# Opening of a fused attention and feed-forward kernel: QKV weight slices in column halves, row 0's mean from two partial sums, rows 1 and 2 turned elsewhere, one residual load moved

## The chip, the cores and the metric

The kernel runs on one core of a Trainium2 chip. A core has TensorE (PE, with its weight loads shown apart as PEld), VectorE (DVE), ScalarE (ACT), GpSimd (POOL) and SyncE (SP), which issues most DMAs; ACT can issue DMAs too. The metric is the device time of one execution in microseconds (us), here the median of three runs.

## The reference, cut to what matters

```python
xn = (x - mean(x)) / sqrt(var(x) + 1e-5)            # x: 2048 x 576, bf16
q, k, v = split(xn @ wqkv)                          # wqkv: 576 x 1728; 32 heads of 18
logits = [q[s] . k[s - 2 w] for w in range(8)] * 18 ** -0.5   # masked where s < 2 w
o = sum(softmax(logits)[w] * v[s - 2 w])
out = x + o @ wo + (silu(xn @ w_gate) * (xn @ w_up)) @ w_down # F = 4608
```

## The kernel before, in words

The 2048 tokens are 16 rows of 128 tokens (token = 16 * partition + row), in four quarters of four rows. The order of all instructions of an engine is the order in which the code issues them (`manual_schedule`); waits between engines are put in by the framework from what each instruction reads and writes.

**Loads (L144 to L165).** `wqkv` is cut along the contraction into slices 0 to 3 of 128 rows and slice 4 of 64 rows, which is kept in two halves of columns, one on partitions 0 to 63, one on 64 to 127. ACT issues row 0 of x and slice 1; SP issues row 1, slice 0, slice 2, row 2, slice 3, slice 4 (two loads), row 3, and then x's chunks 1, 2 and 3 of four rows each (L165). x's chunks lie in the space of `wd`, the QKV weights in that of `hT` (the profile names them so).

**Warm-up (L171).** `warm_pe(n, m)` issues n matmuls of 512 columns and m of 128 on constants. ACT runs a Sqrt ahead (L166), which brings its table load early.

**Layer norm.** `ln_half` (L214) takes bn_stats of 288 of a row's 576 elements, `ln_aggr` (L218) makes mean and variance of both halves, `ln_sqrt` (ACT, L229) and `ln_recip` (L234) the reciprocal deviation, `ln_apply` (L240) the normalized row; POOL or DVE appends a copy of the last 64 elements (L243, L246), so that a row is five tiles of 128. Row 0 is special: it is only centred (`ln_center`, L251; POOL's pad, L256), and its deviation is multiplied in when the products are taken out of PSUM (L365, L367). It is normalized as well, into `xn0`, for later use, and that copy is turned by DMA.

**Turning.** A row's five tiles are transposed by TensorE. For rows 0 and 1 this is `transp_pe` (L262) into PSUM tiles `pa`, `pb` (and `pt1`, the warm-up's bank), copied to SBUF by `copy_pt` (L268). For rows 2 to 4 `transp_halves` (L283, copied at L287) is put in the middle of the matmuls of the row before; later rows are turned by DMA (L291).

**QKV.** A row's products are four PSUM tiles of 432 columns. Row 0 goes slice by slice (`p_whole`, L301): 4 matmuls on slice 0, 4 on slice 1, two on slice 2, then row 1's first three transposes, the other two on slice 2, row 1's last two transposes, then row 1's 4 matmuls on slice 0, and row 0's on slices 3 and 4 (`p_row0_rest`). Later rows use `p_row`: matmuls of half height, two at a time on the two halves of the array, in two passes (`swap`); `at=(i, kt)` says after which step of the second pass the next row is turned. `p_evac` takes the products out, shared between ACT and DVE (L363 to L367).

**After that.** From 60.0 us on, each quarter (`tt`) runs nine chunks (`ch`) of gate and up projections (`g_pair`, L601) with weights `gu` loaded two chunks ahead into two buffers; DVE works on a quarter's attention from a queue of pieces with costs in us (`Filler`). Then come the down projection and `wo` (L630), the residual `xr` is added (L642), and the row is stored. `xr` is loaded at the end of chunk 7 as two DMAs of two rows (L674); `store(2, 3, 3)` writes a buffer of V out in three DMAs at the end of chunk 0 of quarter 0 (L671).

Of the kernel before, what the change touches and what calls it, by code (L numbers as in the profile page):

```python
# [9 lines left out]
bf16 = mybir.dt.bfloat16  # L10
f32 = mybir.dt.float32
ACT = mybir.ActivationFunctionType
ALU = mybir.AluOpType
# [57 lines left out]
def kernel(  # L71
# [75 lines left out]
    def load_w(eng, kt):  # L147
        if kt < 4:
            eng.dma_start(wqkv[:, kt, :], A_wqkv[kt * P:(kt + 1) * P, :])
        else:  # L150
            for i in range(2):
                eng.dma_start(wqkvr[64 * i:64 * i + 64, :], A_wqkv[4 * P:D, 2 * G * i:2 * G * (i + 1)])

    load_x(nc.scalar, 0)
    load_x(nc.sync, 1)
    load_w(nc.scalar, 1)
    load_w(nc.sync, 0)
    make_identity(nc, ident[:])
    load_w(nc.sync, 2)
    load_x(nc.sync, 2)  # L160
    load_w(nc.sync, 3)
    load_w(nc.sync, 4)
    load_x(nc.sync, 3)
    for c in range(1, 4):
        nc.sync.dma_start(xc_b[c], x_v[:, 4 * c:4 * c + 4, :])  # L165
    nc.scalar.activation(warm[:], eps_t[:], ACT.Sqrt)  # L166

    wp = ps.tile([P, 512], f32, name="warm_ps", tag="ps")
    pt1 = wp[:].bitcast(bf16)

    def warm_pe(n, m):  # L171
        one = lambda shape: nc.const_aps.tensor(1.0, shape, bf16)
        for i in range(n):
            nc.tensor.matmul(wp[:].rearrange("p (a b) -> p a b", b=P), one([P, P]), one([P, 4, P]),  # L174
                             start=True, stop=True)
        for i in range(m):
            nc.tensor.matmul(wp[:, 0:P], one([P, P]), one([P, P]), start=True, stop=True)  # L177
# [27 lines left out]
        ln[c] = (xc_b[c], xn_b[c % 2], mv, rstd)  # L205

    sums = {}

    def ln_half(r, k):
        c, j = divmod(r, 4)  # L210
        xc, xn, mv, rstd = ln[c]
        if k == 0:
            sums[r] = lns.tile([P, 2, 6], f32, name="stats")
        nc.vector.bn_stats(sums[r][:, k, :], xc[:, j, k * HALF:(k + 1) * HALF])  # L214

    def ln_aggr(r):
        c, j = divmod(r, 4)
        nc.vector.bn_aggr(ln[c][2][:, j, :], sums[r][:].rearrange("p c s -> p (c s)"))  # L218

    def ln_stats(r, n=1):  # L220
        for i in range(r, r + n):
            ln_half(i, 0)
            ln_half(i, 1)
            ln_aggr(i)

    def ln_sqrt(r, n=1):
        c, j = divmod(r, 4)
        xc, xn, mv, rstd = ln[c]
        nc.scalar.activation(rstd[:, j:j + n], mv[:, j:j + n, 1], ACT.Sqrt, bias=eps_t[:], scale=1.0)  # L229

    def ln_recip(r, n=1):
        c, j = divmod(r, 4)
        rstd = ln[c][3]
        nc.vector.reciprocal(rstd[:, j:j + n], rstd[:, j:j + n])  # L234

    def ln_apply(r):
        c, j = divmod(r, 4)
        xc, xn, mv, rstd = ln[c]
        dst = xn[:, j] if r else xn0
        nc.vector.tensor_scalar(dst[:, 0:D], xc[:, j], mv[:, j, 0:1], rstd[:, j:j + 1],  # L240
                                op0=ALU.subtract, op1=ALU.mult)
        if r < 2:
            nc.gpsimd.tensor_scalar(dst[:, D:DPAD], xc[:, j, 512:D], mv[:, j, 0:1], rstd[:, j:j + 1],  # L243
                                    op0=ALU.subtract, op1=ALU.mult)
        else:
            nc.vector.tensor_copy(dst[:, D:DPAD], dst[:, 512:D])  # L246

    def ln_center(r, lo=0, hi=D):
        c, j = divmod(r, 4)
        xc, xn, mv, rstd = ln[c]  # L250
        nc.vector.tensor_scalar(xn[:, j, lo:hi], xc[:, j, lo:hi], mv[:, j, 0:1], None, op0=ALU.subtract)  # L251

    def ln_center_pad(r):
        c, j = divmod(r, 4)
        xc, xn, mv, rstd = ln[c]
        nc.gpsimd.tensor_scalar(xn[:, j, D:DPAD], xc[:, j, 512:D], mv[:, j, 0:1], None, op0=ALU.subtract)  # L256

    def transp_pe(r, kts, pt):
        c, j = divmod(r, 4)
        xn = ln[c][1]  # L260
        for i, kt in enumerate(kts):
            nc.tensor.transpose(pt[:, i * P:(i + 1) * P], xn[:, j, kt * P:(kt + 1) * P], ident[:])  # L262
# [4 lines left out]
    def copy_pt(eng, r, kts, pt):  # L267
        eng(xT_of(r)[:, kts[0]:kts[-1] + 1, :],  # L268
            pt[:, 0:len(kts) * P].rearrange("p (k t) -> p k t", t=P))
# [34 lines left out]
    def p_whole(r, t, kt, gs=range(NG)):  # L304
        for g in gs:
            p_mm(t, g, kt, None, r, kt == 0, False)
# [14 lines left out]
    def p_row(r, between=None, at=(0, 1), t=None):  # L321


        done = t is not None
        t = t or [None] * NG
        fence = {}
        for swap in range(2):
            for i in range(2):
                for kt in (0, 1, 2, 3) if swap else (0, 4, 1, 2, 3):
                    if done and kt == 0:  # L330
                        continue
                    for half in range(2):
                        g = i + 2 * (half ^ swap)
                        if t[g] is None:
                            t[g] = new_ps("qkv_ps")
                        mm = p_mm(t, g, kt, half, r, swap == 0 and kt == 0, swap == 1 and kt == 3)
                        if swap == 0 and kt == 3 and half == 1:
                            fence[i] = fence_after(mm)
                        if swap and kt == (1 if done else 0) and half == 0:
                            fence_before(mm, fence[i])  # L340
                    if swap and (i, kt) == at and between is not None:
                        between()
        return t
# [36 lines left out]
    def store(m, c, parts=1):  # L380
        st = stage[(2 * c + m - 1) % 4].rearrange("p r d -> p (r d)")
        n = XC // parts
        for i in range(0, XC, n):
            nc.sync.dma_start(kv_d[m - 1, c - 1, :, i:i + n], st[:, i:i + n])
# [89 lines left out]
    def turn(r):  # L474
        return lambda: transp_halves(r)

    warm_pe(10, 1)
    ln_open(0)
    ln_stats(0)
    ln_center_pad(0)  # L480
    ln_center(0, 0, P)
    ln_sqrt(0)
    pa, pb = new_pt(), new_pt()
    transp_pe(0, (0,), pa)
    ln_center(0, P, D)
# [3 lines left out]
    ln_stats(1)  # L489
    ln_sqrt(1)  # L490
    copy_pt(nc.scalar.copy, 0, (3, 4), pb[:, 2 * P:])
    ln_recip(0)
    ln_apply(0)
    ln_recip(1)
    ln_apply(1)

    t = [new_ps("qkv_ps") for g in range(NG)]
    p_whole(0, t, 0)
    p_whole(0, t, 1)
    p_whole(0, t, 2, (0, 1))  # L500
    transp_pe(1, (0, 1), pt1)
    transp_pe(1, (2,), pa)
    copy_pt(nc.scalar.copy, 1, (0, 1), pt1)
    copy_pt(nc.vector.tensor_copy, 1, (2,), pa)
    p_whole(0, t, 2, (2, 3))
    transp_pe(1, (3, 4), pb)
    copy_pt(nc.scalar.copy, 1, (3, 4), pb)
    u = [None] * NG
    for g in (0, 2, 1, 3):
        u[g] = new_ps("qkv_ps")  # L510
        p_whole(1, u, 0, (g,))
    p_whole(0, t, 3)
    p_row0_rest(t)
    ln_stats(2)
    ln_sqrt(2)
    normalize(2)
    p_evac(0, t, (5, 0, 3, 2, 4, 1), dve=(5, 2))
    ln_half(3, 0)
# [1 line left out]
    load_gu(0)  # L520
    transp_dma(0)

    p_row(1, turn(2), (0, 2), u)
    ln_aggr(3)
    p_evac(1, u, (0, 1, 2), dve=(1, 2))
    ln_sqrt(3)
# [120 lines left out]
    for tt in range(NTT):  # L647
        for ch in range(NCH):
            it = tt * NCH + ch
            for p in range(2):  # L650
                g_pair(tt, ch, p)
                for j in (2 * p, 2 * p + 1):
                    g_evac(ch, j)
                    if it % NCH < NCH - 1 or p == 0:
                        dve.pump(1.4)
            if ch == NCH - 1:
                dve.drain(lambda: chains[0] > tt)
                for r in range(RT * tt, RT * tt + RT):
                    nc.sync.dma_start_transpose(oT[:, :, r * P:(r + 1) * P], QOP[:, r, :])
            if it + NSLOT < NTT * NCH:  # L660
                load_gu(it + NSLOT)
            if tt == 0:
                if 1 <= ch <= 7:
                    load_wd(ch - 1)
                if ch == 5:
                    load_wd(8)
                for _ in range(3 if ch in (1, 2) else 2):
                    if wo_order:
                        load_wo(wo_order.pop(0))
                if ch == 0:  # L670
                    store(2, 3, 3)  # L671
            if ch == 7:
                for i in (0, 2):
                    nc.sync.dma_start(xr[:, i:i + 2, :], x_v[:, RT * tt + i:RT * tt + i + 2, :])  # L674
            if ch == 1 and tt < NTT - 1:
                chain(tt + 1)
        for sub in range(0, RT, 2):
            t, fence = {}, {}
            for swap in range(2):
                for i in (sub, sub + 1):  # L680
                    d_half(tt, i, swap, t, fence)
                    if swap:
                        dve.pump(12.5 if i == sub else 4.0)
                        d_out(RT * tt + i, i, t[i])
# [30 lines left out]
```

## Time and profile before

| What | us |
|---|---|
| median of three runs | 504.54 (503.37 to 505.05) |
| the profiled execution, in all | 503.82 |
| its span (first to last instruction) | 502.0 |
| PE busy | 498.1 (99%) |
| PE on gate and up (L601) | 280.4 |
| PE on down projection and wo (L630) | 146.9 + 23.4 |
| PE on QKV, half-height matmuls and others (L301) | 50.2 |
| PE on the warm-up (L174) | 4.4 |
| first matmul on real data (L262, L301) | starts at 5.21, 6.06 |

How to read it: an engine's busy time is the time in which one of its instructions runs. Matmuls overlap, and their ends are modelled, so where PE is busy throughout, the starts of single matmuls say more than the busy share. The chain of waits is followed back from the last instruction. In a timeline, a row is start, length, engine, line, operation, tiles written and read, and in brackets how long the engine had been idle and what released it. In the stretches view, PEclk is the granted clock, the last two columns are the busy share of the DMA engines and what they moved in GB/s.

### The profile page before, as it was taken

What the parts mean: (1) busy time and instruction counts of PE and PEld (TensorE: products, weight loads), DVE (VectorE), ACT (ScalarE), POOL (GpSimd) and SP (SyncE); (2) the same over time, 40 slices, a digit from 0 to 9 for tenths busy, and PEclk for the clock granted to TensorE, in tenths of its full rate; (3) what the DMA queues carried; (4) which work ended last, traced back from release to release, by engine and by line L of the source; (5) the groups of instructions that cost most, each with busy time, mean ns of one, the idle gap of its engine ahead of it and who ended that gap; (6) DMA issues with size and microseconds to landing.
All of it is one profiled execution on the core that took longest, in us unless ns stands there. A gap on an engine that the chain in (4) does not pass through costs nothing.

```text
span 502.0 us, 13267 instructions
## 1 busy us (share of the span) xinstructions
PE 498.1 (99%) x5795; PEld 330.5 (66%) x5795; DVE 329.0 (66%) x478; ACT 200.5 (40%) x415; POOL 2.6 (1%) x9
## 2 busy tenths in 40 slices
PE   9999999999999999999999999999999999999997
PEld 4666655555799755555899655555999555557996
DVE  5888598898999698999898139995980222221001
ACT  4756657644400255554300445557000454553000
POOL 2000000000000000000000000000000000000000
PEclk9999999999999999999999999999999999999999
DMA  8889988789921045536621154465600335453100
GB/s 313 219 206 228 307 280 280 220 273 309 233 82 61 25 136 193 191 106 225 161 69 43 29 185 146 139 189 157 136 25 14 100 114 178 155 177 38 29 14 25
DMA packets 77186, 75.42 MB, mean 150 GB/s; under 512 B 22708, under 2 KB 72528, under 8 KB 77128
## 3 DMA queue, kind: packets, MB, share of 16 engines
q1 hardware_dynamic: 76840, 73.98, 49.7%
q8 instruction: 45, 0.74, 0.6%
q10 hardware_dynamic: 288, 0.59, 0.4%
q14 instruction: 13, 0.11, 0.1%
HBM read 58.76 MB, written 5.90 MB: 129 GB/s over the span
## 4 chain that ended last, share of the span: by engine, by line
PE 99%; DVE 0%; issue 0%
PE g_ps L601 56%; PE d_ps L630 32%; PE qkv_ps L301 11%; PE warm_ps L174 1%; PE pt L262 0%; DVE ot L644 0%; PE pt L283 0%; PE warm_ps L262 0%; PE warm_ps L177 0%
## 5 line engine op out<-in xcount | busy, mean ns | idle before, releaser
L601 PE MATMUL g_ps<-xnT,gu 64*128 64x512 bf16 x2592 | 280.4, 376 | 0.0
L601 PEld LDWEIGHTS <-gu 64*128 64x128 bf16 x2592 | 147.7, 94 | 131.3
L612 ACT ACTIVATE sg<-g_ps 128x512 bf16<-128x512 f32 x144 | 87.3, 606 | 156.6 <-PE g_ps L601 156.6
L630 PE MATMUL d_ps<-wd,hT 64*128 64x288 bf16 x2304 | 146.9, 283 | 0.0
L630 PEld LDWEIGHTS <-hT 64*128 64x128 bf16 x2304 | 131.3, 94 | 10.5
L614 DVE TENSOR_TENSOR hT<-sg,uc 128x512 bf16<-128x512 bf16 x144 | 60.0, 418 | 93.8 <-ACT uc L613 93.6
L613 ACT CAST uc<-g_ps 128x512 bf16<-128x512 f32 x144 | 85.2, 592 | 0.0
L414 DVE TENSOR_REDUCE PP<-PP 128x64 f32<-128x1152 bf16 x64 | 84.9, 1345 | 0.4
L301 PE MATMUL qkv_ps<-hT,xnT 64*128 64x432 bf16 (+1 forms) x536 | 50.2, 343 | 0.0
L409 DVE TENSOR_TENSOR PP<-QO,Kr 128x2304 bf16<-128x2304 bf16 (+1 forms) x35 | 43.5, 1249 | 7.2 <-DMA Kr<-hT 6.9
L642 DVE TENSOR_TENSOR ot<-d_ps,xr 128x288 bf16<-128x288 f32 x30 | 12.3, 451 | 51.1 <-PE d_ps L630 51.1
L441 DVE TENSOR_TENSOR PP<-Vr,A 128x2304 bf16<-128x2304 bf16 (+1 forms) x35 | 43.2, 1250 | 0.4
L301 PEld LDWEIGHTS <-xnT 64*128 64x128 bf16 (+1 forms) x536 | 30.1, 94 | 18.5 <-ACT xnT L287 0.4
L446 DVE TENSOR_TENSOR PP<-PP 128x2304 bf16<-128x2304 bf16 x24 | 32.5, 1353 | 0.3
L612 ACT ACT_TABLE_LOAD x5 | 6.4, 1283 | 47.3 <-PE g_ps L601 47.2
L630 PE MATMUL d_ps<-wo,xnT 64*128 64x288 bf16 x288 | 23.4, 283 | 0.0
L363 ACT CAST hT<-qkv_ps 128x288 bf16<-128x288 f32 (+2 forms) x58 | 21.2, 428 | 0.5 <-DMA kv_d<-hT 0.5
L630 PEld LDWEIGHTS <-xnT 64*128 64x128 bf16 x288 | 16.4, 94 | 1.2
L434 ACT ACTIVATE PP<-PP 128x1024 f32<-128x1024 f32 x4 | 4.2, 1057 | 31.2 <-DVE PP L430 31.2
L644 ACT CAST ot<-d_ps 128x288 bf16<-128x288 f32 x1 | 0.4, 399 | 38.8 <-PE d_ps L630 38.8
L363 ACT CAST QO<-qkv_ps 128x432 bf16<-128x432 f32 (+1 forms) x30 | 12.3, 410 | 7.4 <-PE qkv_ps L301 7.4
L214 DVE BATCH_NORM_STATS2 stats<-wd 128x6 f32<-128x288 bf16 x32 | 12.9, 444 | 2.9 <-DMA wd<-in_A_x_dram 2.6
(53 smaller groups left out, 91.3 us busy)
## 6 DMA issues: line engine op xcount, KB each, us to landing
gu<-in_B_w_gate_dram SPq DMA_DIRECT2D x36, 512.0 KB, 3.8
gu<-in_B_w_up_dram SPq DMA_DIRECT2D x36, 512.0 KB, 5.1
wd<-in_B_w_down_dram SPq DMA_DIRECT2D x9, 576.0 KB, 6.0
kv_d<-hT SPq DMA_DIRECT2D x5, 576.0 KB, 6.4
gu<-in_B_w_gate_dram SPq DMA_DIRECT2D x36, 64.0 KB, 4.7
gu<-in_B_w_up_dram SPq DMA_DIRECT2D x36, 64.0 KB, 4.4
xr<-in_A_x_dram SPq DMA_DIRECT2D x8, 288.0 KB, 5.1
out_dram<-ot SPq DMA_DIRECT2D x16, 144.0 KB, 1.8
```

The costliest lines, as they stand in the source:

```text
L214: nc.vector.bn_stats(sums[r][:, k, :], xc[:, j, k * HALF:(k + 1) * HALF])
L301: return nc.tensor.matmul(t[g][:, 0:G], xT_of(r)[rows, kt, :], w_at(g, kt, rows), start=start, stop=stop)
L363: (nc.vector.tensor_copy if n in dve else nc.scalar.copy)(*parts[n])
L409: nc.vector.tensor_tensor(prod[:, a:b], QO[:, RT * tt + a:RT * tt + b, :], Kr[:, s:s + b - a, :], op=ALU.mult)
L414: nc.vector.tensor_reduce(L[:, w, rs], prod[:, rs].rearrange("p r (h d) -> p r h d", d=DH), axis=AX.X, op=ALU.add)
L441: nc.vector.tensor_tensor(dst[:, a:b], Vr[:, s:s + b - a, :].rearrange("p r (d h) -> p r d h", h=H), A[:, w, a:b].unsqueeze(2).to_broadcas ...
L446: nc.vector.tensor_tensor(dst, acc, pv, op=ALU.add)
L601: mm = nc.tensor.matmul(ring_ps[j][b][:], gu[rows, slot, k, fc], xnT[rows, kt, tok], start=(swap == 0 and kt == 0), stop=(swap == 1 and kt ...
L612: nc.scalar.activation(sg[:], t[0][:], ACT.Silu)
L613: nc.scalar.copy(uc[:], t[1][:])
L614: nc.vector.tensor_tensor(hT[:, ch * FC + j, :], sg[:], uc[:], op=ALU.mult)
L630: mm = nc.tensor.matmul(t[sub][h][:, 0:HALF], a[rows], w[rows, h * HALF:(h + 1) * HALF], start=(swap == 0 and n == 0), stop=(swap == 1 and ...
```

## The change

- Slices 0, 1 and 2 of `wqkv` are each loaded as two DMAs of 128 rows by 864 columns, the left half issued by SP, the right half by ACT, in the order 0, 1, 2. Slice 3, slice 4 and the rows stay on SP. x's chunks 2 and 3 come in one DMA.
- Row 0's mean: ACT copies the left half of the row with a factor 1/576 and sums it, DVE does the same with the right half (`ln_mean0`; the copies go to a scratch area); the centring subtracts both sums. The bn_stats of row 0 (`ln_half(0, ...)`, `ln_aggr(0)`), its Sqrt, reciprocal and normalizing come later, behind row 1's.
- One warm-up matmul of 512 columns less.
- Row 1's transposes: three after row 0's slice 1, all into `pb`, two after three of the four matmuls on slice 2; all its copies on ACT. `ln_stats(2)` and `ln_sqrt(2)` come sooner. Row 2 is turned one step sooner in row 1's second pass.
- Quarter 0's residual is loaded as one DMA of four rows at the end of chunk 0; V's last buffer is stored in two DMAs there instead of three.

```diff
     load_x(nc.scalar, 0)
     load_x(nc.sync, 1)
-    load_w(nc.scalar, 1)
-    load_w(nc.sync, 0)
+    for kt in range(3):
+        for eng, cols in ((nc.scalar, slice(2 * G, 4 * G)), (nc.sync, slice(0, 2 * G))):
+            eng.dma_start(wqkv[:, kt, cols], A_wqkv[kt * P:(kt + 1) * P, cols])
     make_identity(nc, ident[:])
-    load_w(nc.sync, 2)
     load_x(nc.sync, 2)
     load_w(nc.sync, 3)
     load_w(nc.sync, 4)
     load_x(nc.sync, 3)
-    for c in range(1, 4):
-        nc.sync.dma_start(xc_b[c], x_v[:, 4 * c:4 * c + 4, :])
+    nc.sync.dma_start(xc_b[1], x_v[:, 4:8, :])
+    nc.sync.dma_start(wdf[:, 2 * XC:4 * XC].rearrange("p (r d) -> p r d", d=D), x_v[:, 8:16, :])
...
+    def ln_mean0():
+        xc = ln[0][0]
+        nc.scalar.activation(PP[:, 1, 0:HALF], xc[:, 0, 0:HALF], ACT.Copy, scale=1.0 / D, accum_out=part[:, 0:1])
+        nc.vector.tensor_scalar(PP[:, 1, HALF:D], xc[:, 0, HALF:D], 1.0 / D, None,
+                                op0=ALU.mult, op1=ALU.add, accum_out=part[:, 1:2])
...
-        nc.vector.tensor_scalar(xn[:, j, lo:hi], xc[:, j, lo:hi], mv[:, j, 0:1], None, op0=ALU.subtract)
+        nc.vector.tensor_scalar(xn[:, j, lo:hi], xc[:, j, lo:hi], part[:, 0:1], part[:, 1:2],
+                                op0=ALU.subtract, op1=ALU.subtract)
...
-    warm_pe(10, 1)
+    warm_pe(9, 1)
     ln_open(0)
-    ln_stats(0)
+    ln_mean0()
     ln_center_pad(0)
     ln_center(0, 0, P)
-    ln_sqrt(0)
...
     copy_pt(nc.scalar.copy, 0, (3, 4), pb[:, 2 * P:])
-    ln_recip(0)
-    ln_apply(0)
+    ln_half(0, 0)
     ln_recip(1)
     ln_apply(1)
+    ln_half(0, 1)
+    ln_aggr(0)
 
     t = [new_ps("qkv_ps") for g in range(NG)]
     p_whole(0, t, 0)
     p_whole(0, t, 1)
-    p_whole(0, t, 2, (0, 1))
-    transp_pe(1, (0, 1), pt1)
-    transp_pe(1, (2,), pa)
-    copy_pt(nc.scalar.copy, 1, (0, 1), pt1)
-    copy_pt(nc.vector.tensor_copy, 1, (2,), pa)
-    p_whole(0, t, 2, (2, 3))
-    transp_pe(1, (3, 4), pb)
-    copy_pt(nc.scalar.copy, 1, (3, 4), pb)
+    transp_pe(1, (0, 1, 2), pb)
+    copy_pt(nc.scalar.copy, 1, (0,), pb)
+    copy_pt(nc.scalar.copy, 1, (1, 2), pb[:, P:])
+    p_whole(0, t, 2, (0, 1, 2))
+    transp_pe(1, (3, 4), pb[:, 3 * P:])
+    copy_pt(nc.scalar.copy, 1, (3, 4), pb[:, 3 * P:])
+    p_whole(0, t, 2, (3,))
+    ln_sqrt(0)
+    ln_stats(2)
+    ln_sqrt(2)
+    ln_recip(0)
+    ln_apply(0)
...
     p_row0_rest(t)
-    ln_stats(2)
-    ln_sqrt(2)
     normalize(2)
...
-    p_row(1, turn(2), (0, 2), u)
+    p_row(1, turn(2), (0, 1), u)
...
-                    store(2, 3, 3)
-            if ch == 7:
-                for i in (0, 2):
-                    nc.sync.dma_start(xr[:, i:i + 2, :], x_v[:, RT * tt + i:RT * tt + i + 2, :])
+                    store(2, 3, 2)
+            if ch == (7 if tt else 0):
+                n = 2 if tt else RT
+                for i in range(0, RT, n):
+                    nc.sync.dma_start(xr[:, i:i + n, :], x_v[:, RT * tt + i:RT * tt + i + n, :])
```

## The prediction

> **What bounds the kernel now.** I read the page's busy times first, then what TensorE waited for, then the chain that ended last, then the first 16 us engine by engine.
>
> ```profile
> PE 498.1 (99%) x5795; PEld 330.5 (66%) x5795; DVE 329.0 (66%) x478; ACT 200.5 (40%) x415; POOL 2.6 (1%) x9
> ...
> PE 99%; DVE 0%; issue 0%
> ```
>
> PE is busy through the span and is 99% of the chain. Its ends are modelled, so "busy" can hide small stalls; I therefore read the starts of single matmuls in the trace. From 13.93 us to the end no matmul starts more than 0.06 us after the columns of the one before it have passed. The rest of the kernel is thus a fixed sum of matmuls: the change can gain only ahead of 13.93, and must not open a hole behind it. The chain of waits for the first 20 us, start and length:
>
> ```profile
> 0.76 4.42 PE warm_ps L174 x10
> 5.18 0.11 PE warm_ps L177
> 5.29 0.21 PE pt L262
> 5.50 0.02 issue
> 5.52 0.61 PE pt L262 x4
> 6.13 2.25 PE qkv_ps L301 x10
> ```
>
> Real work begins at 6.06 (the first L301). All before it is warm-up and the turning of row 0. The timeline says what row 0 waits for (start, length, instruction):
>
> ```profile
> 3.81 0.82 DVE L214 BATCH_NORM_STATS2 stats<-wd 128x6 f32<-128x288 bf16 x2 [2.63 <-DMA wd<-in_A_x_dram]
> 4.66 0.21 DVE L218 BATCH_NORM_AGGREGATE mv<-stats 128x2 f32<-128x12 f32 x1
> 4.90 0.56 DVE L251 TENSOR_SCALAR wd<-wd,mv 128x128 bf16<-128x128 bf16 x2
> 5.21 0.91 PE L262 MATMUL pt<-ident,wd 128*128 128x128 bf16 x5
> 5.54 0.27 ACT L268 COPY PP<-pt 128x128 bf16<-128x128 bf16 x1 [0.34 <-PE pt L262]
> 6.06 2.31 PE L301 MATMUL qkv_ps<-hT,PP 128*128 128x432 bf16 x10
> ```
>
> Row 0 of x lands at 3.78 (the trace's semaphore times), and the chain is stats, aggregate, centre, turn, copy. The copied tile is loaded into PE at 5.85, yet the matmul starts at 6.06, because slice 0 lands at 6.02. So two things release row 0: this chain and slice 0. The other landings: slice 1 5.74, slice 2 7.16, row 2 7.59, slice 3 9.09, slice 4's halves 9.57 and 9.83. After 6.06, PE loses 0.10 at 8.95 (copies of row 1), 0.10 at 10.52 (the step to half-height matmuls), and 0.14 at 13.73, where weight loads wait for row 2's turned tile:
>
> ```profile
> 13.70 0.51 PEld L301 LDWEIGHTS <-xnT 64*128 64x128 bf16 x8 [0.37 <-ACT xnT L287]
> ```
>
> It also loses to a slow start: warm-up matmuls of 512 columns start 0.427 apart and row 0's first three 0.31 and 0.36 apart, but from 6.93 on 432 columns take 0.182. So PE runs at half its later rate until about 6.7, although the stretches view gives a granted clock of 1.00 there.
>
> **Row 0's mean.** ACT now issues four loads instead of two; an issue takes 0.46 (plus 0.03), so its table load (1.28) moves from 1.64 to about 2.62 and the warm Sqrt ends near 4.12. Starts on ACT overlap by 0.1, so its half of the sum starts at 4.02, not at 3.81. I take 0.40 for it (256-column copies on L268 take 0.35 to 0.37). Writing the sum out is not in this trace: between nothing and one more small ACTIVATE (L229: 0.29); I take 0.15, near the 0.11 to 0.15 of L234. The DVE half (a bn_stats of 288 takes 0.45) is done before. The centring starts at 4.62 instead of 4.90: **0.28 sooner** (0.13 to 0.43). Two scalars instead of one cost nothing there: 576 columns with two (L240) take 0.43, 448 with one 0.39. One warm-up matmul less ends the warm-up at 4.71, before the centring's 4.87, so it hides nothing and costs nothing. Turning and copying follow as before: tile loaded at 5.57, PE free of the other four transposes at about 5.64, first L301 at **5.67, 0.39 sooner, if slice 0 is there**.
>
> **Slices in halves.** The same bytes, slice 0 first instead of 0 and 1 together. In the trace's packets, full-height 3456 B pieces take 135 ns each on a DMA engine, and the first 1728 B pieces 72 ns (later ones 114, below). Per engine, slice 0 is then 16 x 72 = 1.15 us instead of the 2.16 us that slices 0 and 1 take: it lands at 6.02 - 1.01 = 5.01, in time. Slice 1 lands at 6.17 (used from 6.93), slice 2 at 7.38 (used at 7.83). All behind is 3 x 0.072 = 0.22 later: slice 3 at 9.31, slice 4 at **10.05**. An issue waits for the landing of the one eight before it (the semaphore numbers repeat after eight), so SP issues row 2 at 3.8, slice 3 at 4.2, slice 4 at 5.0 and 5.6, row 3 at 6.2, x's chunks at 6.8 and 7.4. Since data flows until 7 by then, the DMA engines do not run dry; behind, gu's first loads start within 0.5 of before, and are used at 60.0. Chunk 2 now lands with chunk 3 (14.5 instead of 13.1), and is read only after row 7's normalizing.
>
> **Row 0 and 1 on PE.** I leave the change of rate at 6.7, since the first warm-up matmul stays at 0.76; at half rate until then, a 0.39 earlier start is worth 0.195. Row 1 is applied by 7.16 and padded by 7.62; PE asks for it at 7.66 and 8.38 (before: 8.21), so turning it sooner costs no stall here. Its copies then lie beside slice 2's three matmuls (0.55), so the 0.10 at 8.95 goes. All three copies are on ACT now, then two Sqrt (0.29 each); row 0's rstd is ready near 9.5 and wanted at 10.2. Slice 3's matmuls start at 9.40 (landed 9.31), slice 4's at 10.23 (landed 10.05) instead of 10.52: **0.29 gained**, with slack of 0.1 and 0.2 left. So slice 4 is next late: even a free row 0 could not bring more than 10.52 - 10.05 = 0.47.
>
> **Row 2 turned one step sooner**: one pair of half-height matmuls (0.183) more lies between its transposes and row 2's first matmul; the stall of 0.137 goes. Its two banks are freed by ACT's copies near 11.9 and wanted at 12.06. **0.14 gained.**
>
> **Residual in the first chunk**: one load of 576 KB at about 72 us instead of two in chunk 7, one store fewer. In the stretches view the DMA engines idle there (75 to 76: share 0.07, 25 GB/s), and gu's next load, issued at 75.8 and landed by 81.3, is wanted at 83.2. Cost 0; without that hole it would take 1.5 of a slack of 1.9.
>
> **Sum**, against the profiled execution (span 502.0, 503.82 in all): 0.195 + 0.095 + 0.14 = 0.43 us, to 503.39. The median of the three runs is 0.72 above it, so 504.54 - 0.43 = **504.1**. At most 0.47 + 0.14 = 0.6; with both bounds of the ACT sum 0.3 to 0.5.
>
> The Trainium skill's "TensorE: Matmul & The Clock Gate", in "Part 1: The HAM clock gate", says the half rate ends at the edge of a free-running window of about 3.4 us, so not by work done. The change of rate 6.0 us after the first matmul allows that (two such windows are an estimate of at most 6.8), and by that rule 0.195 stands; were the rate bound to row 0's third matmul, as the trace allows too, the sum would be 0.39 + 0.095, capped at 0.47, plus 0.14: 0.6.
>
> **Rivals.**
> 1. *Slower: the halves move slowly.* From 8 to 9 us, while slice 4's 1728 B pieces were in flight, the DMA engines were full and moved little (GB/s is the last column):
>
> ```profile
> 7.00:7.50 0.50, 0.50 (x5) 0.25 (x4) 0.43 (x1) 0.02 (x1) 0.50 (x2) 1.00 1.06 415
> 8.00:8.50 0.50, 0.50 (x7) 0.36 (x5) 0.00 (x0) 0.00 (x0) 0.00 (x0) 1.00 1.18 214
> 8.50:9.00 0.50, 0.50 (x6) 0.25 (x4) 0.42 (x2) 0.37 (x1) 0.00 (x0) 1.00 1.08 247
> ```
>
> If that is the size and not the 64-row target, 1.33 MB at 231 instead of 415 GB/s take 5.75 instead of 3.20: slice 4 lands at 12.4, 1.9 after 10.52, less 0.14: 506.3. It decides once slice 4 lands after 10.66 (slower than 330 GB/s). For it: those rows. Against: the first 1728 B pieces took 72 ns, and row 3's 1152 B pieces, too, slowed from 51 to 82 while sharing with slice 4. Chance 0.13.
> 2. *Nothing gained in row 0*: ACT late behind its issues, or slice 3 just late: only 0 to 0.2 goes, 504.4. Chance 0.17.
> 3. *The rate rises later*, since the warm-up is shorter and PE pauses from 4.71 to 4.93. If it needs another stretch as long as the first (6.0, to 12.7), half of that is lost: 507.1. Against: PE pauses in all no longer than before (0.13 + 0.20 + 0.14 there). By the window of 3.4 us that the same page of the Trainium skill gives, an estimate of that loss is 1.7 instead of 3.0, and of the time 505.8. Chance 0.07.
> 4. The forecast, 504.0 to 504.3: 0.63.
>
> A measurement of this kernel can tell about 0.3% (1.5 us) from no change; the three runs lie 1.7 apart. No case gains that much, scatter alone can: faster 0.05. Slower: nearly all of rival 3, a third of rival 1, scatter: 0.12. Within: 0.83. Range: the scatter around 504.1 downwards, 503.1; upwards most of rival 1, 505.8.
>
> **To see afterwards.** Right: first L301 at about 5.7; slice 0 landed by 5.1, slice 4 by 10.1; no weight load waiting for row 2's tile near 13.5; row 1's first L301 near 8.7; nothing new behind 14. Wrong: an ACT half that ends after 4.8; L301 waiting for hT's load at slice 3 or 4; warm-up cadence lasting past 7; or a PE wait behind 60.

## The result, and the profile after

The changed kernel takes 504.44 us (median of 22 runs, 503.92 to 506.11); the kernel before, run beside it, 503.56 (22 runs, 503.27 to 505.05). The ratio is 1.0016, with a 95% interval of 1.0010 to 1.0023: slower by some 0.8 us where 0.43 us less was forecast. (Here and below the ratio is the one on record, which isn't quite the quotient of the two medians.) The time lies in the range on record, but the sign is wrong, and that it is near 504.1 is luck: the median of three runs from which the forecast started, 504.54, was 0.98 above that of the 22.

The profiled execution takes 504.20 in all, with a span of 502.4 (before: 503.82 and 502.0). The first gate matmul starts at 60.37 instead of 60.01, and from there on the two kernels are alike to 0.1 us. So the loss lies ahead of 60 us. The page's busy time of PE and the chain by engine:

```profile
PE 497.5 (99%) x5794; PEld 282.6 (56%) x5794; DVE 329.3 (66%) x479; ACT 201.2 (40%) x418; POOL 2.8 (1%) x9
...
PE 97%; DMA 2%; DVE 0%; SPq 0%; issue 0%
```

DMA, which had no share of the chain before, has 2% of it. The chain of the first 20 us (start, length) says where; no warm-up leads to row 0's products any more, but loads do:

```profile
0.74 2.95 DMA wd<-in_A_x_dram
3.69 0.02 issue
3.71 0.33 SPq L145
4.04 0.04 issue
4.08 6.06 DMA hT<-in_A_wqkv_dram
10.14 0.04 issue
10.19 3.00 PE qkv_ps L309 x26
```

The load issued at 4.08 is slice 3. PE's timeline, with the idle time and its releaser in brackets, shows it and a second wait (slice 1); `L309` is the line of the QKV matmuls now, `L270` that of row 0's and 1's transposes:

```profile
4.93 0.71 PE L270 MATMUL pt<-ident,wd 128*128 128x128 bf16 x5
5.53 0.90 PE L309 MATMUL qkv_ps<-hT,PP 128*128 128x432 bf16 x4
6.95 0.89 PE L309 MATMUL qkv_ps<-hT,PP 128*128 128x432 bf16 x4 [0.52 <-DMA hT<-in_A_wqkv_dram]
7.68 0.33 PE L270 MATMUL pt<-ident,wd 128*128 128x128 bf16 x3
8.02 0.71 PE L309 MATMUL qkv_ps<-hT,PP 128*128 128x432 bf16 x3
8.64 0.27 PE L270 MATMUL pt<-ident,wd 128*128 128x128 bf16 x2
8.93 0.89 PE L309 MATMUL qkv_ps<-hT,xnT 128*128 128x432 bf16 x4
10.19 1.36 PE L309 MATMUL qkv_ps<-hT,PP 128*128 128x432 bf16 x8 [0.36 <-DMA hT<-in_A_wqkv_dram]
```

Since the ends of matmuls are modelled, the brackets show too little; counted from start to start, with 0.182 for 432 columns, PE loses 0.68 ahead of 6.95, 0.17 ahead of 8.02, 0.08 ahead of 8.64 and 0.53 ahead of 10.19. Three of them are landings of slices, which the table below gives from the trace; the 0.08 is row 1's second pair of transposes, which begins when ACT's copies out of the same PSUM tile are done (8.59).

| | forecast | changed kernel | before |
|---|---|---|---|
| slice 0 | 5.01 | 4.98 | 6.02 |
| slice 1 | 6.17 | 6.91 | 5.74 |
| slice 2 | 7.38 | 7.97 | 7.16 |
| slice 3 | 9.31 | 10.14 | 9.09 |
| slice 4 | 10.05 | 10.80 | 9.83 |

The account between the two profiled executions, up to the first gate matmul: first product 0.53 earlier (5.53 for 6.06); its matmuls at the full rate from the start, where before's first two were 0.31 too long together (0.31 and 0.36 apart instead of 0.182), so 0.31 less; losses of 0.68 + 0.17 + 0.08 + 0.53 = 1.46 more; before's stalls of 0.10 (row 1's copies) and 0.14 (row 2's tile) gone. That is -0.53 - 0.31 + 1.46 - 0.24 = +0.38, against 0.36 seen. The 0.31 isn't the change's: the rate rises at another moment in each execution, in this one before 5.5. Without it the profiled loss is 0.67, near the 0.88 between the medians.

### The profile page after: what moved, and what is told of

The parts are those of the page before. It is cut to its first block, busy times and chain, and to the rows that moved or that the text cites. A ratio compares the mean times of both kernels' runs of the same rounds, so it can differ in the third digit from the quotient of the medians.

```text
span 502.4 us, 13268 instructions
## 1 busy us (share of the span) xinstructions
PE 497.5 (99%) x5794; PEld 282.6 (56%) x5794; DVE 329.3 (66%) x479; ACT 201.2 (40%) x418; POOL 2.8 (1%) x9
## 4 chain that ended last, share of the span: by engine, by line
PE 97%; DMA 2%; DVE 0%; SPq 0%; issue 0%
PE g_ps L611 56%; PE d_ps L640 32%; PE qkv_ps L309 10%; DMA hT<-in_A_wqkv_dram 1%; DMA wd<-in_A_x_dram 1%; DVE ot L654 0%; PE pt L291 0%; SPq L145 0%
## 5 line engine op out<-in xcount | busy, mean ns | idle before, releaser
L611 PEld LDWEIGHTS <-gu 64*128 64x128 bf16 x2592 | 126.1, 94 | 152.9
L640 PEld LDWEIGHTS <-hT 64*128 64x128 bf16 x2304 | 112.0, 94 | 29.8
L309 PE MATMUL qkv_ps<-hT,xnT 64*128 64x432 bf16 (+1 forms) x536 | 50.0, 342 | 0.0
L309 PEld LDWEIGHTS <-xnT 64*128 64x128 bf16 (+1 forms) x536 | 26.1, 94 | 22.4 <-ACT xnT L295 0.2
L640 PEld LDWEIGHTS <-xnT 64*128 64x128 bf16 x288 | 14.0, 94 | 3.6
```

The source lines that it names most:

```text
L309: return nc.tensor.matmul(t[g][:, 0:G], xT_of(r)[rows, kt, :], w_at(g, kt, rows), start=start, stop=stop)
L611: mm = nc.tensor.matmul(ring_ps[j][b][:], gu[rows, slot, k, fc], xnT[rows, kt, tok], start=(swap == 0 and kt == 0), stop=(swap == 1 and kt ...
L640: mm = nc.tensor.matmul(t[sub][h][:, 0:HALF], a[rows], w[rows, h * HALF:(h + 1) * HALF], start=(swap == 0 and n == 0), stop=(swap == 1 and ...
```

## The experiments

**Theories at the start.** A: the halved slices land late, and PE waits for them; A1, because two queues feed the same DMA engines; A2, because the pieces are small (1728 B instead of 3456). B: the new order of rows 0 and 1 costs by itself. C: something behind the opening goes wrong, first of all row 5's tile, which is the first that is turned by DMA. Later ones (D, E, F) are told where they came up. "Before" means the kernel before, run beside each on the same chip: medians 503.70 (e1 to e4), 503.76 (e5 to e8), 503.88 (e9 to e12), 503.69 (e13 to e16), 503.71 (e17, e18).

### e1 to e5: the slices, whole and in halves

e1 is the changed kernel with the slices as before:

```diff
-    for kt in range(3):
-        for eng, cols in ((nc.scalar, slice(2 * G, 4 * G)), (nc.sync, slice(0, 2 * G))):
-            eng.dma_start(wqkv[:, kt, cols], A_wqkv[kt * P:(kt + 1) * P, cols])
+    load_w(nc.scalar, 1)
+    load_w(nc.sync, 0)
     make_identity(nc, ident[:])
+    load_w(nc.sync, 2)
```

> The changed kernel, but slices 0, 1 and 2 are loaded whole again, in the queues and order of before (1 on ACT; 0 and 2 on SP). Theory A (the halved loads arrive late: in the changed kernel slices 1 to 4 landed 0.6 to 0.8 us later than worked out, with two of the sixteen DMA engines behind): slice 3 lands by 9.2 and slice 4 by 9.9, no matmul waits for slice 3, and the time is below before, by 0.3 to 0.5 us. Theory B (the new order of row 0's and row 1's work costs the time, whatever the loads do): slower than before by 0.6 to 0.9 us, as the changed kernel is.

e2 is the kernel before with this edit the other way round, so the halves alone.

> The kernel before, with only the halved loads of slices 0, 1 and 2. Theory A: row 0 starts no earlier than 5.9 (its chain is that of before), slices 3 and 4 land near 10.1 and 10.8, row 0's matmuls on slices 3 and 4 wait, and the time is 0.3 to 0.6 us above before. Theory B: within 0.2 us of before, or faster.

e3 is the changed kernel with all six halves issued by SP, e4 with slices 0, 1 and 2 whole, all issued by SP, e5 the changed kernel itself.

```diff
-        for eng, cols in ((nc.scalar, slice(2 * G, 4 * G)), (nc.sync, slice(0, 2 * G))):
+        for eng, cols in ((nc.sync, slice(2 * G, 4 * G)), (nc.sync, slice(0, 2 * G))):    # e3
...
+    load_w(nc.sync, 0)    # e4, for the loop
+    load_w(nc.sync, 1)
+    load_w(nc.sync, 2)
```

> The changed kernel, with all six halves issued by SP, so the pieces are as small as in the changed kernel but one queue holds them all. If the two queues make the DMA engines fall apart (theory A1): all sixteen engines finish a slice within 0.6 us, slice 3 lands near 9.3 and the time is 0.2 to 0.5 us below before. If the small pieces do it (theory A2): slices as late as in the changed kernel, and as slow, 0.6 to 0.9 above before.

> The changed kernel, with slices 0, 1 and 2 whole and all on SP in this order; ACT issues only row 0 of x, so its table load is 1.4 us sooner than in the changed kernel. Theory A1 and A2 alike: slice 0 near 5.0, slice 1 near 6.1, slice 2 near 7.2, slice 3 near 9.1, row 0 starts near 5.5, and the time is 0.3 to 0.6 us below before. Theory B: 0.6 to 0.9 above before.

> The changed kernel once more, beside the others of this call. In its first profile it lost 0.68 us waiting for slice 1, 0.25 for slice 2, 0.53 for slice 3 and nothing for row 5; four variants with earlier starts lost 0.4 to 1.4 us near 24 us, where row 5's matmuls wait for its DMA transpose. Theory A (late slices alone): long DMA packets between 4 and 6 us and 1 us or more of waits for slices again, 0.6 to 1.0 us above before. Theory C (row 5's transpose comes late as well): in some executions a wait near 24 us on top, so a wider spread than before has.

| | median us | ratio to before (95%) | slice 3, slice 4 landed | row 5's tile late by | first gate matmul |
|---|---|---|---|---|---|
| e1 whole, two queues | 504.94 | 1.0023 (1.0014 to 1.0031) | 9.05, 10.01 | 0.9 | 60.51 |
| e2 halves alone | 505.63 | 1.0038 (1.0023 to 1.0052) | 10.48, 11.16 | 0.39 | 61.25 |
| e3 halves, one queue | 505.22 | 1.0023 (1.0010 to 1.0037) | 10.01, 10.81 | 1.41 | 61.66 |
| e4 whole, one queue | 505.11 | 1.0022 (1.0014 to 1.0031) | 10.25, 11.14 | 1.06 | 61.54 |
| e5 changed kernel | 504.98 | 1.0018 (1.0009 to 1.0027) | 10.78, 11.69 | 0 | 61.00 |

Slices 3 and 4 are in time where the loads were as before (e1) and late in every other; the halves alone cost 1.9 us (e2, 0.4 of it at row 5). But neither reading of A holds: one queue is no better than two (e3), and whole slices on one queue, pieces of 3456 B, are as late as halves (e4). What e2 to e5 share is that all DMA engines read one slice (442 KB) at a time, where before and e1 read slices 0 and 1 side by side. That slice 3 is issued later in the changed kernel (4.08 instead of 2.63) isn't it: e4 issued it at 3.07, and it landed at 10.25. The view by stretches shows the price from 5 to 6 us (the last three columns are the granted clock, the DMA engines' busy share and GB/s). Before:

```profile
5.00:6.00 1.00, 0.98 (x7) 0.55 (x6) 1.00 (x4) 0.46 (x2) 0.55 (x1) 1.00 1.06 429
```

The changed kernel, and e4:

```profile
5.00:6.00 1.00, 0.93 (x8) 0.56 (x9) 0.96 (x4) 0.59 (x2) 0.28 (x1) 1.00 1.03 322
```

```profile
5.00:6.00 1.00, 0.92 (x9) 0.54 (x8) 0.96 (x5) 0.64 (x2) 0.19 (x1) 1.00 0.93 256
```

The engines are busy and move a quarter to two fifths less (e16 and e6 below, with the changed kernel's loads, 373 and 394). In the packets it is a few long ones, not a longer usual length: between 2.9 and 7.7 us some 20 to 35 of about 1000 packets in the changed kernel, e2, e3 and e5, and 30 of 625 in e4, take 130 to 1000 ns instead of 72 or 135: 4.6 us of engine time too much in the changed kernel, 10.9 in e5, 9.8 in e3, 7.7 in e4, against 0.3 in before and 1.0 in e1. In the changed kernel 14 of the 16 engines had done their part of slice 1's left half by 6.04 and the last two at 6.85 and 6.91; a load has landed when the last engine is done. The sum over all packets doesn't order the landings, though: of the three later profiles with the same loads, e12 has some 3.6 us too much (slice 4 at 11.17), e16 only 2.0 (10.96) and e6 1.2 (10.13).

The Trainium skill's "DMA: Bandwidth & Descriptors", in "Issuing engines are not separate DMA queues", says that DMAs from several engines end up on the same 16 DMA engines and only save issue time. The traces agree: slice 4 landed at 10.81 with the halves on one queue (e3), at 10.80 and 11.69 with them on two (the changed kernel, e5).

e1 was the surprise: no wait for slices 1 to 4, and still slower by 1.24. Its timeline has another wait:

```profile
24.36 1.82 PE L309 MATMUL qkv_ps<-hT,xnT 64*128 64x432 bf16 x18 [0.73 <-DMA xnT<-wd]
```

That is row 5, whose turned tile landed at 24.32; in before it landed at 22.34 and nobody waited. **Theory D:** row 0's DMA transposes, which go out behind gu(0), meet an instruction fetch of PE (16 KB, the same DMA engines), and everything behind them stands still, row 5's tile too.

### e6 to e8: row 5 ahead of what stood in its way

```diff
-    transp_dma(0)                    # behind load_gu(0)
-    for ring in (Kr, Vr): ...        # zero fills
-    load_wd(7)
     normalize(7)
+    transp_dma(0)
+    for ring in (Kr, Vr): ...
...
                 move(0, ms=(2,))
+                load_wd(7)
```

The edit is made in the changed kernel (e6), in before (e7) and in e1 (e8).

> The changed kernel, but the DMA transpose of row 0, the two zero fills and the load of down-projection chunk 7, which stand ahead of row 5's transpose in SP's queue, are issued behind rows 5 to 7. Theory C: row 5 lands by 21.5, no wait near 24, and the time falls by 0.3 to 0.8 us against the changed kernel. Theory A: the waits for the slices stay, nothing else was there to lose, and the time stays within 0.2 us of the changed kernel.

> The kernel before, with the same four transfers issued behind rows 5 to 7. Before, row 5 landed at 22.3 and was wanted at about 23.3, so both theories: within 0.2 us of before, or up to 0.3 us faster if some of before's executions wait for row 5 too.

> Whole slices in the queues and order of before, the rest as in the changed kernel, and row 5's transpose ahead of the four transfers. Row 0's matmuls ran 0.27 us ahead of before with whole slices, and only the wait of 0.9 us near 24 stood against it. Theory C: that wait goes and the time is 0.3 to 0.5 us below before. If the rest of the change costs time somewhere else (theory B): still 0.5 us or more above before.

Measured: 507.54 (1.0074, 1.0061 to 1.0087), 508.05 (1.0081, 1.0068 to 1.0093) and 509.55 (1.0109, 1.0092 to 1.0127). Row 5 was in time in all three (its tile landed near 22), but the edit only moved the hole, as e6's timeline shows for rows 8 and 10:

```profile
35.37 6.74 PE L309 MATMUL qkv_ps<-hT,xnT 64*128 64x432 bf16 x72 [1.66 <-DMA xnT<-wd]
43.78 2.54 PE L309 MATMUL qkv_ps<-hT,xnT 64*128 64x432 bf16 x26 [1.66 <-DMA xnT<-wd]
```

The control e7 lost as much, so these three say nothing on the change.

### e9, e10, e12: the two heavy items moved to row 10; e11: two slices at once, in small pieces

```diff
     load_gu(0)
-    transp_dma(0)
...
-    load_wd(7)
...
+        if r == 10:
+            transp_dma(0)
+            load_wd(7)
```

in e1 (e9), in before (e10), in the changed kernel (e12). e11 is the changed kernel with slice 0 in two halves on SP beside slice 1 in two halves on ACT, then slice 2 whole on SP:

```diff
-    for kt in range(3):
-        for eng, cols in ((nc.scalar, slice(2 * G, 4 * G)), (nc.sync, slice(0, 2 * G))):
+    for cols in (slice(0, 2 * G), slice(2 * G, 4 * G)):
+        for eng, kt in ((nc.scalar, 1), (nc.sync, 0)):
             eng.dma_start(wqkv[:, kt, cols], A_wqkv[kt * P:(kt + 1) * P, cols])
     make_identity(nc, ident[:])
+    load_w(nc.sync, 2)
```

> Slices 0 to 2 whole as before (0 and 2 on SP, 1 on ACT), the rest of the change kept, and row 0's DMA transposes and the eighth load of wd moved from the opening to row 10's turn of the loop (the zero fills stay). Theory D (row 5's turned tile is late because row 0's DMA transposes stand in front of it while PE's instruction fetch passes): row 5's tile lands by 22.5, no wait for it, first gate matmul near 59.6, and 0.2 to 0.5 us less than before. Theory B (the new order of rows 0 and 1 costs by itself): at least 0.5 us more than before, with no wait for row 5.

> The kernel before with the same two items moved to row 10's turn. Theory D: within 0.2 us of before, since row 5's tile was in time there. If the move itself costs, it shows here as a wait for a later row's tile, and is taken off from the run beside it.

> The changed kernel with slice 0 in two column halves on SP, slice 1 in two column halves on ACT, so that two slices are read at once as in before, and slice 2 whole on SP. If it is the reading of one slice by all engines at a time that makes packets long: the time of packets beyond their usual length sums to under 1.5 us, slice 3 lands by 9.4, slice 4 by 10.2, and no wait of PE for a slice. If it is the small pieces: 4 us or more of such excess, slice 4 after 10.7, and waits as in the changed kernel.

> The changed kernel with row 0's DMA transposes and the eighth load of wd moved to row 10's turn. No wait for row 5's tile. If slices 1 to 4 are late again (slice 4 after 10.6), the time is within 0.3 us of the changed kernel's; if they are in time, 0.3 to 0.8 us less than it.

e9 has no wait for row 5, as D says, and its first gate matmul comes at 59.40, 0.61 ahead of before's profile. Not all of that is the change's: e10, without the change, reaches it at 59.71, and e15 below, before with two lines exchanged, at 59.47. Before's own profile had a slow opening, as its first products show. Against these controls the rest of the change shows no clear gain in the opening (e14, e17 and e18 below: 59.42 to 59.67), and not the loss of 0.6 to 0.9 of B either. The time of e9 is worse all the same, 506.07 (1.0054, 1.0034 to 1.0074): from the first gate matmul to the first down projection it needs 71.29 us instead of before's 69.93, with waits near 92. e10 needs 71.71 there, waits at 76.7 for a gate weight load, and takes 505.29 (1.0023, 1.0014 to 1.0033) instead of at most 0.2 more; e12 needs 71.88 and takes 506.21 (1.0046, 1.0033 to 1.0060). So the move costs, and the totals don't decide.

e11 came out between the two answers: 2.3 us of packet time too much, slice 3 at 9.81, slice 4 at 10.53, PE waits of 0.59 and 0.30 for slices and 1.0 for row 5, 504.80 (1.0024, 1.0015 to 1.0034). Its long packets are mostly those of slice 2, from 5.08 on. It doesn't settle why packets get long.

### e13 to e16: row 0 turned ahead of gu(0)

No byte goes to a later place this time; two lines change places:

```diff
+    transp_dma(0)
     load_gu(0)
-    transp_dma(0)
```

e13 is e1 with x's chunks in three loads again, without that edit; e14 is e13 with it, e15 before with it, e16 the changed kernel with it. **Theory E** was for another riddle. e1's first gate matmul was 0.5 later than before's, its time 1.24 longer, and its last output store landed 2.5 us after its issue instead of 1.75: perhaps a matter of how many pieces SP's queue had carried.

> The changed kernel with slices 0 to 2 whole as before, and x's chunks loaded in three DMAs as before, so one DMA more on SP than the run with whole slices (e1). Theory E (the last store's late engine belongs to the number of pieces on SP's queue): the last store lands 1.75 us after its issue, not 2.5, and the time is 0.4 to 0.6 us above before, by the wait for row 5's tile alone. If the late engine belongs to whole slices: it lands after 2.5 us again, and the time is 1.1 to 1.4 above before.

> As e13, and row 0's DMA transposes issued ahead of gu(0) instead of behind it. Theory D (those transposes meet PE's instruction fetch behind gu(0) and all DMA engines then stand still for 1.5 us): row 5's tile lands by 23, no wait for it, first gate matmul near 59.5, and 0.3 to 0.6 us less than before. If the instruction fetch alone delays the stream, row 5's tile is still late (after 23.5), and the time is as e13's.

> The kernel before with row 0's DMA transposes ahead of gu(0). Theory D: within 0.2 us of before, since its row 5 was in time. If SP's wait for row 0's normalized copy (until about 11.6) delays gu(0) or row 5 instead, a wait of PE behind 20 us shows it, and the time is above before.

> The changed kernel, slices in halves, with row 0's DMA transposes ahead of gu(0). Slices 1 to 4 late as in the changed kernel (slice 4 after 10.6) and no wait for row 5's tile: 0 to 0.4 us less than the changed kernel, 0.4 to 1.0 above before. If the lateness of the slices cost nothing in the end, it would come out at e14's time.

| | median us | ratio to before (95%) | slice 4 landed | row 5's tile landed | first gate matmul |
|---|---|---|---|---|---|
| e13 | 504.96 | 1.0023 (1.0014 to 1.0033) | 9.88 | 24.08 | 60.27 |
| e14 | 504.27 | 1.0011 (1.0002 to 1.0020) | 9.77 | 22.52 | 59.42 |
| e15 | 503.93 | 1.0001 (0.9992 to 1.0010) | 9.71 | 22.23 | 59.47 |
| e16 | 504.21 | 1.0009 (1.0000 to 1.0018) | 10.96 | 23.55 | 60.39 |

The exchange took the wait for row 5 away (e14). The DMA view of 17 to 20 us (the DMA engines' share in tenths, and GB/s, in 40 slices of 0.075 us), first of e13, with row 0's transposes behind gu(0):

```profile
DMA  9999999943999999000000000010100100499599
GB/s 202 273 239 249 239 219 410 116 75 85 261 353 334 338 307 31 0 0 0 0 0 0 0 3 7 7 10 10 15 0 15 15 15 0 138 399 169 15 46 46
```

then of e14:

```profile
DMA  9999999999999968999984614379989999999999
GB/s 355 341 355 355 328 341 356 532 301 355 314 293 200 231 169 292 215 246 230 169 31 29 31 14 44 31 91 137 184 198 244 323 369 307 415 323 353 292 292 307
```

Each slice counts the packets that begin in it. PE's instruction fetch begins at 17.49 and 17.52 and takes 1.31 and 1.13. In e13 it falls among row 0's transposes (pieces of 256 B): all but 11 of the 640 have begun by 17.95, the last 11 begin only from 18.8 to 19.1, when the fetch is over, and meanwhile 19 of the next packets (1152 B), begun by 18.15, take 1.5 us instead of 0.05. From 18.2 to 19.5 hardly a packet begins. In e14 gate weights (1024 B) stand in that place and are done by 17.9; the packets behind them take 0.6 at most, and row 5's tile comes 1.56 sooner. The other profiles bear D out: packets of over 1 us within 1 us of that fetch, 16 to 27 of them, stand in the six in which PE waited for row 5 (e1 to e4, e11, e13), and none in the other fourteen. In before, with the transposes behind gu(0) too, only 19 of the 640 pieces were left when the fetch began (18.01), in e13 over 200. That the other engines wait for the one that carried the fetch is what these times suggest; it isn't shown. PE at row 5, e13 and then e14:

```profile
24.12 2.18 PE L309 MATMUL qkv_ps<-hT,xnT 64*128 64x432 bf16 x22 [0.52 <-DMA xnT<-wd]
```

```profile
21.82 4.36 PE L309 MATMUL qkv_ps<-hT,xnT 64*128 64x432 bf16 x46
```

The control e15 is level with before, and e16 takes 0.5 more than before (the interval just touches 1) with its slices late and row 5 in time; its first gate matmul comes 0.97 after e14's. So late slices cost by themselves.

E fell: e13 has another number of pieces on SP's queue and the same late store. And e14 took 0.6 more than before, though 0.3 to 0.6 less was expected. Two things took it away: PE lost 0.39 at 83.1, where a gate weight load was late,

```profile
83.12 1.85 PEld L611 LDWEIGHTS <-gu 64*128 64x128 bf16 x18 [0.51 <-DMA gu<-in_B_w_up_dram]
```

and the last store again landed 0.63 late.

### e17 and e18: the two losses that were left

**Theory F:** in all of the profiles with a late last store, and in no other, an 8 KB instruction fetch falls within that store, 1.0 us after its issue, on one of the DMA engines. All these kernels have 578 instructions on ACT. With 574 to 577 the last fetch came after the end (502.5 or later), with 579 and 580 at about 478 to 481.

```diff
-            if ch == (7 if tt else 0):          # e17: e14 with the residual as before
-                n = 2 if tt else RT
+            if ch == 7:
...
-                    store(2, 3, 2)
+                    store(2, 3, 3)
...
+            for i in range(3):                  # e18: e17 and, in row 12's turn of the loop
+                nc.scalar.copy(warm[:], eps_t[:])
```

> As e14, and quarter 0's residual and the store of V's last buffer as in before. If the load of the residual in the first chunk is what holds the gate weights: no wait at 83 us, first down projection at most 69.95 us after the first gate matmul as in before. Theory F (ScalarE's instruction fetch meets the last store): ScalarE has 578 instructions still, so the last store lands some 2.4 us after its issue, and the time is 0.1 to 0.4 above before.

> As e17, with three copies of one element per partition added on ScalarE in row 12's turn of the loop, off the chain that sets the end. Theory F: 581 instructions, the fetch falls before 480 us, the last store lands 1.75 us after its issue, and the time is 0.65 us below e17's, 0.2 to 0.5 below before. If the fetch is not the cause: as e17.

e17: 504.10 (1.0007, 0.9998 to 1.0017). e18: 503.55 (0.9998, 0.9989 to 1.0007). Three copies whose result nobody reads made the kernel 0.55 us faster than e17 (0.65 expected). The DMA view of the last 5.5 us, e17 and then e18 (q14 carries that fetch; the last column of an issue is its time to landing):

```profile
q1 hardware_dynamic: 144, 0.15, 7.5%
q14 instruction: 1, 0.01, 0.7%
...
out_dram<-ot SPq DMA_DIRECT2D x1, 144.0 KB, 2.3
```

```profile
q1 hardware_dynamic: 144, 0.15, 7.5%
...
out_dram<-ot SPq DMA_DIRECT2D x1, 144.0 KB, 1.7
```

Over all profiles the last piece of that store ended 1.96 to 2.09 us after the issue in the six kernels with 578 instructions, and 1.37 or 1.38 in the other fourteen. The wait at 83 us is gone in both; one profile each shows that, and e17 put back two things at once, the residual's load and the store of V's last buffer, so it doesn't show which of them it was.

e18 is the best version found, and no faster than before by what this measurement can tell, where 0.2 to 0.5 less was expected. With it B falls too, a loss of 0.6 to 0.9 by the new order: e18 contains the new mean, the new order of rows 1 and 2 and the shorter warm-up.

## Why the prediction was wrong, step by step

- **Slices in halves: this step failed.** Slice 0 came as forecast (4.98 for 5.01), by the packet length of 72 ns. To carry that length on for slices 1 and 2 was wrong: they were 0.74 and 0.59 late, slices 3 and 4 0.83 and 0.75. The usual length did stay at 72; what the sum lacked were a few packets of up to 1000 ns, and the engine with the most of them sets the landing. I had weighed piece size (rival 1), not that before's rows all come from two slices read side by side. The point that rival 1 named, slice 4 landing after 10.66, was crossed (10.80), and the side it gave is the one that came; its cause, small pieces, isn't needed: e4 is as late with pieces of 3456 B. Over twenty profiles slice 4 landed between 9.71 and 10.01 in the eleven with slices 0 and 1 whole on two queues, at 10.53 in e11, and between 10.13 and 11.69 in the eight that read one slice after another. The step's own slack of 0.1 and 0.2 was too thin for that. e6, with the same loads, landed slice 4 at 10.13 and lost nothing to a slice: the forecast's landing times can occur, but don't as a rule.
- **Row 0's mean: right.** ACT and DVE lines of the changed kernel:

```profile
4.01 0.43 ACT L211 ACTIVATE PP<-wd 128x288 bf16<-128x288 bf16 x1
4.34 0.19 ACT L211 ACTIVATION_READ_ACCUMULATOR PP<-wd 128x1 f32 x1
4.56 0.62 DVE L257 TENSOR_SCALAR wd<-wd,part 128x128 bf16<-128x128 bf16 x2 [0.39 <-ACT PP L211]
```

  The half started at 4.01 (forecast 4.02), writing the sum out took 0.19 (0.15), the centring began at 4.56 (4.62), the first product at 5.53 (5.67). But it needs slice 0 early, and so the loads that failed: with whole slices the first product waits for slice 0, landed at 5.79 in e18.
- **Row 0 and 1 on PE: wrong.** Of the 0.29 to be gained at slice 4, 0.49 was lost instead (its matmuls at 11.01, before 10.52), by the slices. And the stall at row 1's copies doesn't go where slices are in time: in e18 it is 0.245 at 8.25 instead of 0.10, since the second pair of transposes goes into the PSUM tile that ACT is still copying from (until 8.20). The wait for slice 0 and the start of that pair in e18:

```profile
5.83 1.62 PE L309 MATMUL qkv_ps<-hT,PP 128*128 128x432 bf16 x8 [0.34 <-DMA hT<-in_A_wqkv_dram]
...
8.25 0.27 PE L270 MATMUL pt<-ident,wd 128*128 128x128 bf16 x2
```

- **The change of rate at 6.7 and the 10.52 to gain on: taken from one execution.** The rate was up before 5.5 in the changed kernel's profile, so the halving of 0.39 to 0.195 had no ground there. And before's profile is the slow one: in e7, e10 and e15, before with edits that only come later, slice 4's matmuls start at 10.22, 10.21 and 9.98. Against these, a slice 4 landing at 10.05 as forecast leaves 0 to 0.17 to gain there, not 0.29.
- **Row 2 turned one step sooner: right.** No stall is left at its tile, and e2, without this edit, still has 0.14.
- **Residual in the first chunk: right here, by luck.** The slack it needs is there while PE is late; 1 us earlier (e14) it cost 0.39.
- **"Nothing new behind 14": right for the changed kernel, for a bad reason.** I followed the DMA stream only to gu, used at 60, and left out row 5's tile, wanted at 23.4. The forecast's own gain, had it come, would have run into that wait, as e1 and e13 did.
- **Rivals 2 and 3.** The rate rose no later than before, so 3 didn't happen. Rival 2's "slice 3 just late" understated it.

No run has all of the 0.43: e18, with the slices in time and the later losses gone, is 0.16 below before between medians, within the scatter, but its first product waits for slice 0. Still open: why most kernels that read one 442 KB slice at a time meet long packets, why their number changes from run to run, and the share of each cause in unprofiled runs.

## What to carry to other kernels

A usual packet length doesn't tell when a load has landed: the slowest of 16 engines does, and a few long packets set it. Leave slack for that, above all when the order of loads changes. Look at more than one profile of the kernel before: its opening alone varied by 0.54 (first gate matmul between 59.47 in e15 and 60.01), more than the gain that was sought. When PE is moved forward, follow every load that is wanted behind the place, not only the ones that the change touches, and look at what the instruction fetches land on. Differences of half a microsecond need a control with an idle edit beside them, since the number of instructions alone shifted the end by 0.55 here.

## What the runs showed of the hardware

- PE's instruction fetches are 16 KB (queue q8, 45 in each profile; that they are PE's is an inference from its 11600 instructions) and take 0.9 to 2.2 us (2.18 in e3). One among DMA transposes had 19 packets of other loads take 1.5 us (e13); beside plain loads it was 0.6 at most (e14). The Trainium skill's "Runtime: NRT & Kernel Launch", in "Instruction fetch mechanics", has each engine fetch its next block of 16 KiB over DMA and calls the cost mostly hidden. The traces agree on PE's size and on the DMA engines, not on the cost: here it was 0.4 to 1.4 us at row 5, where the fetch met transposes, and, by an 8 KB fetch, 0.55 at the last store. That the latter is ACT's is an inference from the instruction counts.
- Writing out an accumulated sum is an instruction of its own: 0.19 on ACT, 0.08 on DVE.
- The matmul rate rose to its full value between about 3.9 us (e3: 512 columns begin 0.427 apart, then 0.313 from 3.71 and 0.221 from 4.02) and 6.7 us (before, e6) in different executions, though the granted clock reads 1.00 throughout. First products between 5.5 and 6.1 thus cost 0 to 0.5 us more or less by chance (e6: three of them 0.36 apart instead of 0.182), as much as all the gains forecast here.
